# A three-layer kernel on one core: when weights are decoded, how the last part of `wo` is multiplied, and where weight parts are kept

## The chip, the cores and the metric

The kernel runs on one core of a Trainium2 chip. The metric is the device time of one execution in microseconds. Five engines of the core matter here: TensorE (PE) multiplies, VectorE (DVE), ScalarE (ACT) and GpSimd (POOL) work on tiles elementwise, and SyncE (SP) starts the transfers. Each engine takes its instructions strictly in the order in which they were written, and waits on semaphores for the others.

## The reference

Three steps follow each other, for 2 batches of 448 tokens:

```
scores = q @ k.T / 8, causal mask, softmax, @ v          # 12 heads of 64, per batch
x  = attn / sqrt(mean(attn^2) + 1e-6) * rms_g            # 896 x 768
x  = (silu(x @ w_gate) * (x @ w_val)) @ w_out            # 768 -> 1536 -> 768
y  = relu(x @ w_in)^2 @ w_out2                           # 768 -> 2048 -> 768
```

The weights come as 64-bit floats and the result is a 32-bit float.

## The kernel before, in words

**Numbers.** A weight tile (128 x 768 of 64-bit words, tile `raw`) is decoded on the core: ACT makes the exponent part (L639) and the lowest bits (L644), DVE puts the number together (L649). Then each 32-bit weight and each activation is split in two parts for PE: the high part is a rounded copy (L267 on ACT, L265 on POOL) and the low part is the rest (a subtraction: L676 for weights, on DVE or POOL; L559 for activations). A split weight of three 128 x 128 blocks lives in one of the buffers `ring`, a split activation in a `part`. One product of blocks is three matmuls (high x high, high x low, low x high), so a product of three blocks is 9 matmuls of 128 x 448 (L691).

**Products.** Each layer's matrix products work on pairs of output columns and both batches. `halves` does a pair with seven block products in place of eight (Strassen-Winograd): 7 x 9 = 63 matmuls, with sums of weight quarters (`minus`, L703, tiles `st`) and sums of activation quarters (`differences`, L723) in front, and additions behind. `whole` does a pair of output columns in the plain way: 2 columns x 2 batches x 2 x 9 = 72 matmuls. `wg` and `wv` (gate and value, ten `halves` after two plain columns), `wo` in two halves of its depth, then `w2i` (eight `halves`) and `w2o` follow.

**Attention.** Twelve pairs of heads run first. Per pair PE makes scores (L359, L363, L372, L375) in two PSUM tiles `s`, DVE takes maxima (L405, L403), ACT exponentials (L430), DVE reciprocals (L445, L446), POOL multiplies the rows (L456), PE transposes (L472), ACT or DVE copies the transposed rows out of PSUM (`pt<-t`, L308), and PE multiplies by the values (L505, L510). The squares of the result are summed (L535, L540) for the norm, whose column sums are PE's L573 and whose row broadcast is L592. The first four weight tiles of `wg` and `wv` are decoded while the attention runs, into the tiles `wt`. Their matmuls for batch 0 (L895) use the PSUM tiles of the scores.

**Order.** All work is given to a planner (class `Order`) as steps with a due time, the engines that may do it and how long each takes. The planner goes through time in its own model: it takes the step that can begin first, and of those within SLACK of it the one that is due first. A step with a choice goes to the engine on which begin + duration + COST is least; DVE pays PORT in place of its COST where the step is marked `port` (both operands in SBUF, which DVE and POOL are not planned to do together) and is not yet close to due (EASY, EARLY). SOON is how much earlier than a product's due time the step that clears its bank is due. What the planner leaves is a fixed order on each engine; on the chip only semaphores decide when an instruction runs.

Of the kernel before, what the change touches and what calls it, by code (L numbers as in the profile page):

```python
# [8 lines left out]
F32 = mybir.dt.float32  # L9
F32R = mybir.dt.float32r  # L10
BF16 = mybir.dt.bfloat16
U32 = mybir.dt.uint32
# [5 lines left out]
B, H, S, D = 2, 12, 448, 64  # L18
DM, DF1, DF2 = 768, 1536, 2048
P = 128  # L20
CP = 64
NCH = S // CP
NCC = DM // P
NF1 = DF1 // P
NF2 = DF2 // P
NPAIR = H // 2
# [3 lines left out]
CN = 112  # L30
NE = 2
STRIDE = 5.5
SLACK = 0.1
SWITCH = 0.1
SOON = 12.0
COST = {"D": 0.4, "P": 0.4}
PORT = 1.0
EASY = 1015
EARLY = 8
LAT = {"S": 0.0}  # L40
NEXT = 0.05
SPARE = 0.15
# [144 lines left out]
def tile_attention_moe_moe2(ctx: ExitStack, tc: tile.TileContext, qk, v, wg, wv, wo, w2i, w2o, rms_g, out):  # L187
# [16 lines left out]
    pw = ctx.enter_context(tc.tile_pool(name="pw", bufs=1))  # L204
# [5 lines left out]

    shapes = dict(raw=([P, 6 * P, 2], U32), wt=([P, 6 * P], F32), st=([P, 3 * P], F32), ring=([P, 6 * P + 64], F32R),
                  snap=([P, S], F32), tt=([P, S], F32), uu=([P, S], F32), part=([P, 2, S], F32R), row=([P, S], F32),
                  s=([P, 1024], F32))
    order = Order(dict(qk=3, v=3, p1=2, p2=2, pt=2))
    add, chain, buf = order.add, order.chain, order.buf

    def have(pool, **n):
        for name, k in n.items():  # L220
            for _ in range(k):
                i = len(order.places.get(name, ()))

                def make(name=name, i=i):
                    t = pool.tile(shapes[name][0], shapes[name][1], tag=f"{name}{i}", name=name, bufs=1)
                    if name == "ring":

                        o = 63
                        t = t[:, o:o + 6 * P].rearrange("p (a k n) -> p a k n", a=2, k=3)
                    return t  # L230

                order.more(name, make)

    def banks(name, *which):
        for i in which:
# [2 lines left out]
    have(psum, s=2)  # L238
    banks("t", 0, 1, 2)
    banks("o", 3)  # L240
    have(pw, raw=2, wt=2, st=4, ring=8)
    have(pt_, snap=5, tt=2, uu=2, part=6, row=14)


# [35 lines left out]
    for i, fill in enumerate((1.0, -1.0e9 * float(D) ** 0.5)):  # L280
        for k in range(2):
            for sl in (slice(0, D), slice(D, P)):
                t = half[sl, 2 * i + k]
# [8 lines left out]
    for i in range(NV):  # L292
        t = atc.tile([P, 4, 2 * D], F32, name=f"vt{i}")
# [3 lines left out]
    for i in range(2):  # L297
        t = atc.tile([P, 2, 512], F32, name=f"p2t{i}")
# [251 lines left out]
    def parts(src, due, prev=(), bs=None):  # L550

        bf, t, new = src[0], src[1], [] if bs else [buf("part")]
        bs = bs or new[0]

        def high(e):
            rnd(E(e), bs.tile[:, 0], bf.tile)

        def low(e):
            E(e).tensor_sub(bs.tile[:, 1], bf.tile, bs.tile[:, 0].bitcast(F32))  # L559

        t = add(due, {"A": A_(S), "P": P_(S)}, high, [t], new=new, uses=[bf] if new else [bf, bs], prev=prev)
        return bs, add(due, {"P": P_(S, True), "D": D_(S)}, low, [t], uses=[bf, bs], port=True)
# [235 lines left out]
    hf = [[None] * NF1, [None] * NF1]  # L798
# [107 lines left out]
        have(p, part=18, row=18)  # L906

    add(0.0, {"X": 0.0}, rows_come, used)
    norm(0, (NPAIR + 3.5) * STRIDE, 8.0)
    norm(1, 0.0, 0.3)  # L910
    ws = []
    for k in range(2 * NE):
        due = 40 + 8.0 * k
        c, t = weights((wg, wv)[k % 2][k // 2], NCC, due, due, "wt")
        ws.append([form((c, o, t), 3, due) for o in (0, 3 * P)])
    whole_tiles(0, ws, 1000.0)
# [8 lines left out]
    due = 1020.0  # L925
# [36 lines left out]
    def halved(x, k0, prev=(), both=False):  # L962

        x = [y[k0:k0 + NCC] for y in x]
        f = dict(B11=[parts(x[0][j], due - 6 + j, prev) for j in range(3)],
                 B21=[parts(x[0][j + 3], due - 5 + j, prev) for j in range(3)])
        f.update(differences(x, due - 4, prev, both))
        f.update(B22=[parts(x[1][j + 3], due + j + 6, prev) for j in range(3)])
        return f

    def highs(f):
        return [x[1] for y in (f.values() if isinstance(f, dict) else f) for x in y]
# [22 lines left out]
    def seven(src, k0, f, sums, due, last=False, n=NCC // 2):  # L995


        for a in range(n):
            c = (a, a + NCC // 2)
            own = [[sums[j][c[i]] for i in range(2)] for j in range(B)]  # L1000

            def done(i, j, bank, snap, after, due, keep, c=c, own=own):
                t = kept(own, i, j, bank, snap, after, due, c[i] if last else None)
                sums[j][c[i]] = own[j][i]
                return t

            halves(src[c[0]][:, k0:k0 + NCC], src[c[1]][:, k0:k0 + NCC], f, due, done,
                   sums=own if own[0][0] else None, end=last and a == NCC // 2 - 1)
            due += 12.8
        return due  # L1010

    def whole(src, k0, n, x, sums, due, a0=0):

        for a in range(a0, NCC):
            c = a // 2 + a % 2 * NCC // 2
            layer(src[c], x, k0, [n], due, lambda b, bank, t, due, c=c: kept(sums, c, b, bank, None, [t], due))
            due += 1.22 * n * 2
        return due
# [2 lines left out]
    g = halved(hf, 0, highs(f))  # L1021
    due = seven(wo, 0, g, yf, due)
    hx = halved(hf, NCC, highs(g))
    due = seven(wo, NCC, hx, yf, due, n=NCC // 2 - 1)
    hy = [[parts(hf[1][NCC + i], due - 5 + i, highs(hx)) for i in range(3)]]
    due = whole(wo, NCC, NCC, [hx["B11"] + hx["B21"], hy[0] + hx["B22"]], yf, due, NCC - 2)
    f = halved(yf, 0, highs(hy))
    h2 = [[None] * NF2, [None] * NF2]

    def squared(b, ft, bank, snap, after, due, keep=False):  # L1030
# [77 lines left out]
```

## Time and profile before

| what | value |
|---|---|
| runs before | 555.04, 553.03, 550.48 us; median 553.03 |
| profiled execution | 552.47 us, span 550.7 us, so 1.8 us lie around the span |
| mean granted clock of PE | 0.996 |
| busy in the span | PE 540.6, PE weight load 477.3, DVE 420.2, ACT 411.0, POOL 301.8 us |
| matmuls of L691 | 2115, 429.4 us busy |
| bytes | 65.06 MB by DMA, mean 118 GB/s |

A matmul's end in the trace is modelled, so PE's busy share hides short waits: what counts is when matmuls start. A row of the timeline merges instructions of one kind that follow each other without a wait, with the start of the first and their count; the time from one row's start to the next row's start is what they took in all.

### The profile page before, as it was taken

Reading aid. Unit: us, or ns where it says so; the run is one execution under the profiler, and the core shown is the slowest. Engines: PE = TensorE matmul, PEld = TensorE weight load, DVE = VectorE, ACT = ScalarE, POOL = GpSimd, SP = SyncE. Lnnn points to the kernel's source line nnn. Section 1 sums busy time; section 2 is a strip of 40 time slices with the busy share of each in tenths; the row PEclk is TensorE's granted clock in tenths of the full one; section 3 lists DMA queues with packets and bytes.
Section 4 is the critical chain, followed back from the end, with each engine's and each line's share of the span. In section 5 each row is a group of like instructions: output and inputs, shape, how many; then the busy total and the mean of one; then the engine's idle time right before and its main releaser. Section 6 shows DMA issues by size and latency. Waiting matters only on the chain.

```text
span 550.7 us, 8919 instructions
## 1 busy us (share of the span) xinstructions
PE 540.6 (98%) x3067; PEld 477.3 (87%) x3067; DVE 420.2 (76%) x781; ACT 411.0 (75%) x879; POOL 301.8 (55%) x338
## 2 busy tenths in 40 slices
PE   8999999999999999999999999999999999999997
PEld 5776666798899999999999989899899999999996
DVE  3667867699999897889867877996777544778883
ACT  3889989656867766679888776888887998659610
POOL 3555555325232372248999789231113897899810
PEclk9999989999999999999999999999999999999999
DMA  7246514023144333333544153243332343333422
GB/s 184 86 140 191 166 55 132 0 78 130 57 147 165 116 115 115 114 116 114 170 140 149 58 174 115 62 156 128 114 117 77 114 154 114 115 115 116 148 85 83
DMA packets 19501, 65.06 MB, mean 118 GB/s; under 512 B 2048, under 2 KB 8960, under 8 KB 19456
## 3 DMA queue, kind: packets, MB, share of 16 engines
q1 hardware_dynamic: 19376, 64.27, 35.8%
q8 instruction: 24, 0.39, 0.3%
q10 hardware_dynamic: 80, 0.23, 0.1%
q14 instruction: 21, 0.17, 0.1%
HBM read 61.74 MB, written 2.75 MB: 117 GB/s over the span
## 4 chain that ended last, share of the span: by engine, by line
PE 74%; DVE 13%; ACT 6%; DMA 3%; issue 2%; POOL 1%; POOLq 0%; DVEq 0%; ACTq 0%
PE m L691 61%; DVE part L559 3%; PE t L472 3%; PE o L510 3%; PE s L359 3%; DVE ring L676 2%; DMA raw<-in_w2i 2%; PE s L372 2%; DVE row L723 1%; PE s L895 1%; ACT ring L267 1%; ACT p2t L430 1%; DVE s L649 1%; POOL p L456 1%; ACT s L639 1%
## 5 line engine op out<-in xcount | busy, mean ns | idle before, releaser
L691 PE MATMUL m<-part,ring 128*128 128x448 f32 x2115 | 429.4, 365 | 1.4 <-ACT ring L267 0.6
L691 PEld LDWEIGHTS m<-part,ring 128*128 128x128 f32 x2115 | 396.9, 188 | 33.8 <-ACT ring L267 1.2
L559 POOL TENSOR_TENSOR part<-row,part 128x448 fp32r<-128x448 f32 x103 | 121.5, 1204 | 50.6 <-ACT part L267 47.3
L676 DVE TENSOR_TENSOR ring<-s,ring 128x384 fp32r<-128x384 f32 (+1 forms) x156 | 82.3, 541 | 39.1 <-ACT ring L267 38.3
L267 ACT CAST ring<-s 128x384 fp32r<-128x384 f32 (+1 forms) x156 | 71.5, 471 | 23.8 <-PE m L691 14.8
L267 ACT CAST part<-row 128x448 fp32r<-128x448 f32 x131 | 69.1, 571 | 6.8 <-DVE row L611 2.6
L723 POOL TENSOR_TENSOR row<-row 128x448 f32<-128x448 f32 x57 | 66.3, 1179 | 12.3 <-DVE row L835 11.4
L644 ACT ACTIVATE raw<-raw 128x768 uint32<-128x768 uint8 (+1 forms) x70 | 62.5, 895 | 13.9 <-DMA raw<-in_w2o 4.5
L265 POOL TENSOR_SCALAR ring<-st 128x384 fp32r<-128x384 f32 x14 | 7.4, 527 | 100.9 <-PE m L691 48.6
L639 ACT ACTIVATE s<-raw 128x768 f32<-128x768 f32 (+1 forms) x64 | 54.0, 853 | 7.9 <-DVE ring L676 6.4
L649 DVE SCALAR_TENSOR_TENSOR s<-s,raw 128x768 uint32<-128x768 uint32 (+1 forms) x64 | 48.8, 762 | 10.9 <-ACT s L639 5.9
L676 POOL TENSOR_TENSOR ring<-st,ring 128x384 fp32r<-128x384 f32 x45 | 45.9, 1038 | 5.0 <-ACT ring L267 3.7
L456 POOL TENSOR_SCALAR p<-p,r 128x128 f32<-128x128 f32 (+1 forms) x48 | 24.0, 517 | 27.0 <-DVE r L446 25.1
L267 ACT CAST ring<-st 128x384 fp32r<-128x384 f32 x44 | 21.5, 515 | 23.0 <-DVE st L703 22.4
L405 DVE TENSOR_REDUCE mx<-s 128x2 f32<-128x256 f32 (+2 forms) x36 | 24.1, 688 | 17.9 <-PE s L375 11.2
L703 DVE TENSOR_TENSOR s<-s,st 128x384 f32<-128x384 f32 x56 | 31.6, 564 | 1.6
L456 POOL TENSOR_SCALAR p2t<-p2t,r 128x256 f32<-128x256 f32 (+1 forms) x36 | 23.1, 658 | 17.3 <-DVE r L446 7.3
L703 DVE TENSOR_TENSOR st<-st,s 128x384 f32<-128x384 f32 x56 | 30.5, 545 | 0.2
L359 PE MATMUL s<-qk 64*128 64x128 f32 (+2 forms) x144 | 26.4, 448 | 1.6 <-ACT p2t L430 1.1
L981 DVE TENSOR_TENSOR row<-m,row 128x448 f32<-128x448 f32 x36 | 22.3, 618 | 6.7 <-PE m L691 6.4
L308 ACT COPY snap<-m 128x448 f32<-128x448 f32 x43 | 22.8, 530 | 5.2 <-PE m L691 5.0
L559 DVE TENSOR_TENSOR part<-row,part 128x448 fp32r<-128x448 f32 x37 | 25.3, 708 | 0.9 <-ACT part L267 0.8
(101 smaller groups left out, 564.4 us busy)
## 6 DMA issues: line engine op xcount, KB each, us to landing
raw<-in_w2i SPq DMA_DIRECT2D x16, 768.0 KB, 4.2
raw<-in_wg SPq DMA_DIRECT2D x12, 768.0 KB, 4.5
raw<-in_wv SPq DMA_DIRECT2D x12, 768.0 KB, 4.3
raw<-in_wo SPq DMA_DIRECT2D x12, 768.0 KB, 4.3
raw<-in_w2o SPq DMA_DIRECT2D x12, 768.0 KB, 4.5
qk<-in_qk SPq DMA_DIRECT2D x11, 448.0 KB, 4.0
raw<-in_w2o SPq DMA_DIRECT2D x6, 512.0 KB, 3.7
out_t<-row SPq DMA_DIRECT2D x12, 224.0 KB, 1.9
```

Of the source, the lines that this page charges most:

```text
L267: eng.copy(o, i)
L359: nc.tensor.matmul(s[:, h, o:o + n], z["qk"][BOTH[h], 0, qs], z["qk"][BOTH[h], 1, :n], start=True, stop=False)
L405: nc.vector.tensor_reduce(z["mx"][:, k:k + 2], src, AX, ALU.max)
L456: E(e).tensor_scalar(t, t, z["r"][:, k:k + 1], 1.0, ALU.mult, ALU.mult)
L559: E(e).tensor_sub(bs.tile[:, 1], bf.tile, bs.tile[:, 0].bitcast(F32))
L639: nc.scalar.activation(bt.tile[:, :n * P], br.tile[:, :n * P, 1].bitcast(F32), AF.Prelu, scale=2.0 ** -112, alpha=2.0 ** 32)
L644: nc.scalar.activation(br.tile[:, :n * P, 0], b, AF.Copy, scale=1.0 / 32, bias=-31.0 / 64)
L649: nc.vector.scalar_tensor_tensor(dst.tile.bitcast(U32) if dst else u, u, 3, br.tile[:, a:b, 0], ALU.logical_shift_left, ALU.bitwise_or)
L676: E(e).tensor_sub(br.tile[:, 1, :n], num(), br.tile[:, 0, :n].bitcast(F32))
L691: nc.tensor.matmul(bank.tile[:, :S], bw.tile[:, a, i], x[:, c], start=first and i == 0 and k == 0, stop=last and i == n - 1 and k == 2, sk ...
L703: (E(e).tensor_add if plus else E(e).tensor_sub)(bs.tile[:, o:o + 3 * P], x, y)
L723: E(e).tensor_sub(bs.tile, a[0].tile, b[0].tile)
```

## The change

It has four parts. The planner's numbers are others (eight of them, and some due times). The four early weight tiles are due at 26, 41, 56 and 71 of the planner's time in place of 40, 48, 56 and 64, and the norm of batch 0 is due at 55 in place of 52.25. The last two columns of `wo`'s second half, before a `whole` of 72 matmuls, become a third `halves` of 63. There are nine buffers `ring` in place of eight, cut from one tile `rings`, and three tiles `st` in place of four.

```diff
-SLACK = 0.1
+SLACK = 0.15
...
-COST = {"D": 0.4, "P": 0.4}
-PORT = 1.0
+COST = {"D": 0.3, "P": 0.4}
+PORT = 1.1
...
-    have(pw, raw=2, wt=2, st=4, ring=8)
+    have(pw, raw=2, wt=2, st=3)
+
+    NR = 9
+    rings = pw.tile([P, NR * 6 * P + 64], F32R, name="rings")
+    for i in range(NR):
+        order.more("ring", lambda i=i: rings[:, 63 + i * 6 * P:63 + (i + 1) * 6 * P].rearrange("p (a k n) -> p a k n", a=2, k=3))
...
-    norm(0, (NPAIR + 3.5) * STRIDE, 8.0)
+    norm(0, (NPAIR + 4) * STRIDE, 7)
...
-        due = 40 + 8.0 * k
+        due = 26 + 15 * k
...
-    due = seven(wo, NCC, hx, yf, due, n=NCC // 2 - 1)
-    hy = [[parts(hf[1][NCC + i], due - 5 + i, highs(hx)) for i in range(3)]]
-    due = whole(wo, NCC, NCC, [hx["B11"] + hx["B21"], hy[0] + hx["B22"]], yf, due, NCC - 2)
-    f = halved(yf, 0, highs(hy))
+    due = seven(wo, NCC, hx, yf, due)
+    f = halved(yf, 0, highs(hx))
```

The lines of the kernel move up by three to five with it (L676 becomes L673, L308 becomes L305). Counted over the whole program PE has 9 instructions fewer, ACT 37 fewer, POOL 36 fewer and DVE 68 more; the transfers are the same 121. The moves between engines that make up these counts are: low parts of weights in `st` on POOL 45 before and 11 now, on DVE 13 and 49; copies `pt<-t` on ACT 41 and 20, on DVE 7 and 28; the last `relu` and square of `w2i`'s tiles on ACT (two instructions each) 23 and 10, on DVE (one) 9 and 22.

The first place is DVE in the middle of the attention, from a copy of a pair's result to the reciprocals of the next but one. Before:

```order
L308 COPY row<-o 128x448
L405 TENSOR_REDUCE mx<-s 128x2
L445 TENSOR_SCALAR r<-su 128x4
L446 RECIPROCAL r<-r 128x4
L403 TENSOR_REDUCE mx<-s 128x1
L308 COPY pt<-t 128x2x2x128
L405 TENSOR_REDUCE mx<-s 128x2
L540 TENSOR_TENSOR snap<-snap,tt 128x448
L405 TENSOR_REDUCE mx<-s 128x2
L445 TENSOR_SCALAR r<-su 128x3
L446 RECIPROCAL r<-r 128x3
```

And now:

```order
L305 COPY row<-o 128x448
L402 TENSOR_REDUCE mx<-s 128x2
L442 TENSOR_SCALAR r<-su 128x4
L443 RECIPROCAL r<-r 128x4
L400 TENSOR_REDUCE mx<-s 128x1
L305 COPY pt<-t 128x2x2x128
L305 COPY pt<-t 128x2x4x64
L402 TENSOR_REDUCE mx<-s 128x2
L537 TENSOR_TENSOR snap<-snap,tt 128x448
L402 TENSOR_REDUCE mx<-s 128x2
L442 TENSOR_SCALAR r<-su 128x3
L443 RECIPROCAL r<-r 128x3
```

DVE has taken a second copy `pt<-t` between the maxima, which ACT did before.

The second place is POOL in the stage of `wg` and `wv`, up to the nine differences for `wo`. Before:

```order
L265 TENSOR_SCALAR ring<-st 128x384
L676 TENSOR_TENSOR ring<-st,ring 128x384
L723 TENSOR_TENSOR row<-row 128x448 x2
L265 TENSOR_SCALAR ring<-st 128x384
L676 TENSOR_TENSOR ring<-st,ring 128x384
L265 TENSOR_SCALAR ring<-st 128x384
L676 TENSOR_TENSOR ring<-st,ring 128x384 x2
L265 TENSOR_SCALAR ring<-st 128x384
L676 TENSOR_TENSOR ring<-st,ring 128x384 x2
L723 TENSOR_TENSOR row<-row 128x448 x9
```

And now:

```order
L720 TENSOR_TENSOR row<-row 128x448
L556 TENSOR_TENSOR part<-row,part 128x448 x3
L720 TENSOR_TENSOR row<-row 128x448 x2
L262 TENSOR_SCALAR rings<-st 128x384 x2
L720 TENSOR_TENSOR row<-row 128x448 x9
L262 TENSOR_SCALAR rings<-st 128x384
L673 TENSOR_TENSOR rings<-st,rings 128x384
```

The subtractions for the low parts in `st` have left POOL here; they stand on DVE.

The third place is PE at the column sums of batch 0's norm. Before, they stand between the scores of the tenth pair:

```order
L363 MATMUL s<-both 128x64
L573 MATMUL o<-ones,snap 112x1 x4
L359 MATMUL s<-qk 128x256 x2
```

```order
L472 MATMUL t<-ident,p_968 128x128 x8
L505 MATMUL o<-pt,vt_119 64x128 x2
```

And now, one pair earlier, in front of a transpose:

```order
L360 MATMUL s<-both 128x64
L570 MATMUL o<-ones,snap 112x1 x4
L469 MATMUL t<-ident,p_864 128x128 x8
L502 MATMUL o<-pt,vt_118 64x128 x2
L507 MATMUL o<-pt,vt_118 64x320 x4
L507 MATMUL o<-pt,vt_118 64x192 x2
L507 MATMUL o<-pt,vt_118 64x64 x2
L356 MATMUL s<-qk 128x256 x2
```

The sums moved from behind the eighth pair's transposes to behind the seventh's, and no scores follow them directly.

## Rows read from the trace of the kernel before

**Rows 1.** The page's first part: busy us (share of the span) and instructions by engine.

```profile
PE 540.6 (98%) x3067; PEld 477.3 (87%) x3067; DVE 420.2 (76%) x781; ACT 411.0 (75%) x879; POOL 301.8 (55%) x338
```

**Rows 2.** Busy time by stretch: length, then busy us (instructions) by engine, granted clock, DMA.

```profile
core 0: us, PE busy (x) PEld busy (x) DVE busy (x) ACT busy (x) POOL busy (x), PEclk, DMA share, GB/s
20.00:38.00 18.00, 18.00 (x185) 13.15 (x180) 10.61 (x26) 15.27 (x54) 9.13 (x18) 1.00 0.29 88
38.00:64.00 26.00, 25.10 (x248) 17.30 (x248) 19.96 (x43) 24.34 (x76) 14.45 (x27) 1.00 0.60 192
...
112.00:160.00 48.00, 47.52 (x236) 43.77 (x235) 47.83 (x87) 34.45 (x66) 18.84 (x16) 1.00 0.28 97
160.00:260.00 100.00, 100.00 (x499) 93.35 (x498) 87.47 (x157) 71.88 (x132) 41.43 (x42) 1.00 0.39 127
...
386.00:494.00 108.00, 107.81 (x523) 98.58 (x522) 68.58 (x126) 86.56 (x166) 69.81 (x66) 1.00 0.35 117
```

**Rows 3.** PE's timeline in the stream: start, us, instruction xcount [idle before <-releaser].

```profile
116.48 18.56 PE L691 MATMUL m<-part,ring 128*128 128x448 f32 x92
135.28 12.61 PE L691 MATMUL m<-part,ring 128*128 128x448 f32 x61 [0.24 <-DVE ring L676]
148.12 169.84 PE L691 MATMUL m<-part,ring 128*128 128x448 f32 x846 [0.23 <-ACT ring L267]
318.37 67.65 PE L691 MATMUL m<-part,ring 128*128 128x448 f32 x333 [0.41 <-ACT ring L267]
386.21 161.05 PE L691 MATMUL m<-part,ring 128*128 128x448 f32 x783 [0.19 <-ACT snap L308]
```

**Rows 4.** Busy time and counts of L691's matmuls alone, in two stretches of the stream.

```profile
268.00:308.00 40.00, 40.00 (x201) 37.56 (x200) 1.00 0.37 120
...
400.00:440.00 40.00, 40.00 (x195) 36.59 (x194) 1.00 0.32 106
```

**Rows 5.** PE's timeline at the value products of pairs two to six.

```profile
26.68 0.44 PE L505 MATMUL o<-pt,vt 128*64 128x128 f32 x4
...
33.58 0.44 PE L505 MATMUL o<-pt,vt 128*64 128x128 f32 x4
...
48.22 0.44 PE L505 MATMUL o<-pt,vt 128*64 128x128 f32 x4
...
54.39 1.22 PE L472 MATMUL t<-ident,p 128*128 128x128 f32 x8 [0.23 <-POOL p L456]
55.54 0.44 PE L505 MATMUL o<-pt,vt 128*64 128x128 f32 x4
```

**Rows 6.** PE's timeline from 71 us, behind the sums of batch 0's norm.

```profile
71.00 0.70 PE L359 MATMUL s<-qk 64*128 64x256 f32 x4 [1.10 <-ACT p2t L430]
...
71.71 1.89 PE L472 MATMUL t<-ident,p 128*128 128x128 f32 x8
73.53 0.69 PE L505 MATMUL o<-pt,vt 128*64 128x128 f32 x4
...
76.25 0.97 PE L372 MATMUL s<-qk 64*64 64x224 f32 x8
```

**Rows 7.** PE alone by stretches of 2 us: busy us (instructions), granted clock, DMA.

```profile
72.00:74.00 2.00, 2.00 (x12) 0.50 0.00 2
74.00:76.00 2.00, 2.00 (x16) 0.68 0.00 0
```

**Rows 8.** Groups by shape: busy us, mean ns of one | idle us before, by releaser.

```profile
L676 DVE TENSOR_TENSOR ring<-s,ring 128x384 fp32r<-128x384 f32 x150 | 80.9, 551 | 38.4 <-ACT ring L267 37.6
L676 DVE TENSOR_TENSOR ring<-st,ring 128x384 fp32r<-128x384 f32 x13 | 8.1, 650 | 0.0
L308 DVE COPY pt<-t 128x512 f32<-128x512 f32 x7 | 4.8, 680 | 1.1 <-PE t L472 1.1
L1044 DVE SCALAR_TENSOR_TENSOR row<-row 128x448 f32<-128x448 f32 x9 | 5.6, 619 | 0.2
...
L676 POOL TENSOR_TENSOR ring<-st,ring 128x384 fp32r<-128x384 f32 x45 | 45.9, 1038 | 5.0 <-ACT ring L267 3.7 <-PE m L691 0.2
```

More of the change, by code (lines that the diff above doesn't have):

```diff
@@ L32 @@
 STRIDE = 5.5
-SLACK = 0.1
+SLACK = 0.15
 SWITCH = 0.1
-SOON = 12.0
-COST = {"D": 0.4, "P": 0.4}
-PORT = 1.0
-EASY = 1015
-EARLY = 8
+SOON = 14.0
+COST = {"D": 0.3, "P": 0.4}
+PORT = 1.1
+EASY = 1020
+EARLY = 5
 LAT = {"S": 0.0}
@@ L209, in tile_attention_moe_moe2 @@
     atc = att.enter_context(tc.tile_pool(name="atc", bufs=1))
-    shapes = dict(raw=([P, 6 * P, 2], U32), wt=([P, 6 * P], F32), st=([P, 3 * P], F32), ring=([P, 6 * P + 64], F32R),
+    shapes = dict(raw=([P, 6 * P, 2], U32), wt=([P, 6 * P], F32), st=([P, 3 * P], F32),
                   snap=([P, S], F32), tt=([P, S], F32), uu=([P, S], F32), part=([P, 2, S], F32R), row=([P, S], F32),
@@ L222, in have @@
                 i = len(order.places.get(name, ()))
[L224 to L232, printed above, removed]
+                order.more(name, lambda name=name, i=i: pool.tile(shapes[name][0], shapes[name][1], tag=f"{name}{i}",
+                                                                   name=name, bufs=1))
     def banks(name, *which):
```

## The prediction, made before the changed kernel was run

> **What bounds the kernel now.** I read the page's first part, then the busy time by stretch, then PE's own timeline.
>
> The first part shows PE at 98% of the span, and no other engine over 76% [rows 1]. A matmul's end is modelled, so the 98% alone proves little. The timeline counts starts. From 116.48 us to the end PE runs one stream of 2115 matmuls, which waits only four times [rows 3]. Its longest part, 846 matmuls from 148.12 to 318.37 us, takes 201.2 ns for each. Nothing but fewer or denser matmuls shortens that. The last part is less dense without any wait: 783 matmuls in 161 us, 205.6 ns each, 3.4 us more than at 201.2. Inside it the same instruction of the same shape starts 195 times in 40 us, where an earlier stretch has 201, both at a granted clock of 1.00 [rows 4]. So PE has two cadences. The slower one began after the wait at 386.21 us, and no instruction of the program is special to it.
>
> The attention, up to about 105 us, has another limit. From one pair's value product to the next PE takes 33.58 - 26.68 = 6.90 us early on, and 55.54 - 48.22 = 7.32 us later, where it waits for POOL's row factors [rows 5]. In that later stretch ACT is busy 24.34 of 26 us (94%), in the earlier one 15.27 of 18 (85%), while DVE has 77% and 59% [rows 2]. The decoding of early weights has come on top of ACT's exponentials, and POOL waits at the end of that chain. Behind the norm's sums PE waits another 1.10 us for ACT's exponentials to free a PSUM tile [rows 6], and then its clock falls: 0.50 of full speed, which is its lower level of 1.2 GHz, over 72 to 74 us, and 0.68 as a mean over the next two [rows 7].
>
> **The change, part by part.** The sum starts from the profiled execution, 552.47 us; the median of the three runs, 553.03, is 0.6 above it, and I add nothing for that.
>
> *Seven products for the last two columns of `wo`.* 63 matmuls in place of 72: 9 x 0.2012 = 1.8 us less on PE [rows 3], on the path since the stream is dense. What it costs is work elsewhere: three more weight parts, four more sums of weights, three more additions behind the products, and less slack before `w2i`. Before, four products of the next pairs (36 matmuls, 7.2 us) lie in PE's order between the last product of `wo` and the first that needs all of its columns; now three (5.4 us). Over that time DVE has about ten instructions of 0.55 to 0.62 us in its order (the shapes of [rows 8]), 6 us at the middle. This could cost PE up to 0.7 us or nothing; I take nothing, since POOL and ACT share the chain.
>
> *The attention.* Decoding goes from one weight in 8 of the planner's units to one in 15, and 21 copies `pt<-t` go from ACT to DVE. At 680 ns each [rows 8] that is 14.3 us more on DVE over twelve pairs, 1.2 us in each pair's 6.9. DVE's 59% without decoding becomes some 76% by the copies and ACT loses about as much, so neither is near the 94% at which the waits stood. I count as gone: four pairs that took 0.42 us too long, 1.7 us; the wait of 1.10 us; and the time at the lower clock, (1 - 0.50) x 2 + (1 - 0.68) x 2 = 1.6 us [rows 5 to 7]. Together 4.4. The other bound is a loss: the norm's sums need the sixth pair's squares, and stand less than a pair's period behind its value product now, before more than one and a half. If nothing is won and PE waits here as it did for the exponentials, it is +1.1. I take -4.4, because the stretch from 20 to 38 us shows this very loop without waits at ACT's 85%.
>
> *Low parts from POOL to DVE.* 36 subtractions move; at 551 ns alone they are 19.8 us of DVE, against 36 x 1.038 us of POOL given back [rows 8]. In the stage of `wg` and `wv`, 12 of them move (13 stand on POOL there before, 1 now): 6.6 us. DVE's load from 112 to 260 us goes from 47.83 + 87.47 = 135.3 to 141.9 of 148 us [rows 2]: 96%, which fits, narrowly. What a full DVE does to PE is seen from 116.48 to 148.12 us, where DVE is at 99.6%: 153 matmuls take 31.64 us, 0.9 more than at 201.2 ns [rows 3]. Spread over 148 us this would be 4.1, of which 0.9 is there already. I take +1.5, between 0 and 3.2. In `w2i`'s stage DVE has 68.58 of 108 us [rows 2]; the 13 squares (619 ns) and some ten low parts add 14 us and stay at 76%, so I cost them at nothing, with DVE's own idle time as the cover.
>
> Beside this: `st,ring` on DVE takes 650 ns as a mean where `s,ring`, whose first operand lies in PSUM, takes 551 [rows 8]. The Trainium skill (GPSIMD Engine Reference, section Specifications) says that GpSimd shares its SBUF interfaces with VectorE and contends with instructions that read two SBUF operands, which speaks against this move. By that rule each moved subtraction is priced at the 650, and DVE would get 3.6 us more in all.
>
> *Nine buffers in one tile, three `st`.* One more buffer lets the parts run 9 matmuls further ahead. In the built program each write to a buffer waits for the matmul that read that same slice last, so the common tile couples nothing. The waits it can spare are among the four of the stream, and the tile `st` that is missing can cost as much. I put it at 0.
>
> *The cadence.* Each wait seems to draw it anew, and of four waits one led to the slow one. In the likeliest case the stream runs at 201 throughout and 3.4 us go; but the runs before spread over 4.6 us, so a median probably holds some of it. I take half, -1.7, with 0 and -3.4 as its near bounds.
>
> The sum: 552.47 - 1.8 - 4.4 + 1.5 - 1.7 = 546.1. I predict **546 us**, 1.3% below the median.
>
> **Rivals.**
>
> *The waits move with the work (22%).* The copies and the early decoding put DVE's reciprocals later, and POOL waits for those instead of for ACT. For it: POOL's factors need DVE's result, and DVE is in order. Against: 76% is far from 94%. Then the attention gives nothing: 552.5 - 1.8 + 1.5 - 1.7 = 550.5.
>
> *DVE becomes the bound (13%), slower than before.* Place: 112 to 260 us. DVE is already at 99.6% for the first 48 us, and the change brings it more backlog out of the attention. If its 12.5 us of idle time in 160 to 260 are waits that it can't fill, then the 12 moved subtractions lie on the path, 6.6 us, and the attention's gain is only backlog passed on: 552.5 - 1.8 + 6.6 = 557.3. It decides from the point where DVE's load reaches what PE takes, 12.7 us for 63 matmuls. The Trainium skill (Perfetto Trace Analysis, section Identifying the Most-Contended Engine) takes busy time as a fair measure for VectorE but not for matmuls, where the weight loads count. By that rule DVE (47.83 of 48 us) and not PE (43.77) is the engine to relieve from 112 to 160 us, and this rival would be the forecast; the trace agrees for 48 us only, since in the next 100 it has 87.47 against 93.35.
>
> *The stream falls into the slow cadence early (6%).* With few waits left there is nothing to end it. 195 against 201 starts is 3.1%, over 2106 matmuls 13.1 us, of which 3.4 are there now: 546.1 + 1.7 + 9.7 = 557.5.
>
> *The tile does couple its buffers (2%).* Every decoding would wait for the latest product: far above 600 us. The program's waits speak against it.
>
> **How the numbers follow.** The forecast has 57%, with 542 (all of the cadence, no price on DVE) to 550 as its own range. A measurement here can tell about 1% from no change: 547.5 and 558.6 are the bounds. Faster: three quarters of the forecast and a little of the first rival, 44%. Slower: a third of the two rivals at 557, and the last, 10%. The rest, 46%, is within 1%. The range that leaves out 2 in 10 goes from 541.5, a little under the forecast's best case since two waits of PE in the attention weren't counted, to 557.
>
> **What would show it.** The changed profile should have 2106 matmuls of 128 x 448 in the stream; pairs 6.9 us apart through the whole attention, with the first matmul of the stream 4 us earlier; no stretch of clock below 1 after the start; DVE near 96% from there for 150 us and PE without long waits on DVE's low parts; and 201 starts in any 40 us of the stream. I am wrong if PE's waits in the attention carry DVE's name, if the stream shows many waits for `rings` released by DVE, or if it starts 195 times in 40 us for long.

## The result and the profile after

The changed kernel is slower: **555.04 us** median of 20 runs, against 548.82 us for 20 runs of the kernel before that were taken beside it. The ratio is 1.0088, 95% interval 1.0065 to 1.0111. I had forecast 546. The ratio leaves out four of the 20 runs: 752 and 1857 us (mean granted clock 0.655 and 1.000; why is not known), and 559 and 561 us, which are over 1.5% above the fastest. The profiled execution took 555.26 us, that of the kernel before 552.47, which turns out to be one of its slower ones.

The page's first part, beside [rows 1]: DVE has 37 us more, ACT 19 and POOL 39 us less, and PE 4 us less.

```profile
PE 536.6 (97%) x3058; PEld 473.6 (86%) x3058; DVE 457.3 (83%) x849; ACT 392.3 (71%) x842; POOL 263.2 (48%) x302
```

Busy time by stretch, with the columns of [rows 2]:

```profile
38.00:64.00 26.00, 25.00 (x248) 17.58 (x248) 21.40 (x48) 22.87 (x75) 13.93 (x28) 1.00 0.48 157
112.00:160.00 48.00, 45.56 (x226) 41.98 (x225) 47.48 (x85) 31.57 (x61) 15.36 (x13) 1.00 0.24 83
160.00:260.00 100.00, 100.00 (x501) 93.91 (x501) 93.80 (x172) 72.85 (x136) 32.15 (x32) 1.00 0.39 130
```

DVE is full to 160 us as before, and at 94% behind it, where it had 87%. PE does not suffer in that second stretch: 100.00 of 100 us. It does in the first (45.56 for 47.52), and beyond 260 us. PE's timeline of the stream, beside [rows 3]:

```profile
114.00 26.81 PE L688 MATMUL m<-part,rings 128*128 128x448 f32 x133
141.72 2.47 PE L688 MATMUL m<-part,rings 128*128 128x448 f32 x11 [0.90 <-DVE part L556]
145.72 122.68 PE L688 MATMUL m<-part,rings 128*128 128x448 f32 x612 [1.54 <-DVE row L807]
270.21 88.28 PE L688 MATMUL m<-part,rings 128*128 128x448 f32 x432 [1.81 <-ACT snap L305]
359.41 136.01 PE L688 MATMUL m<-part,rings 128*128 128x448 f32 x657 [0.92 <-DVE row L1029]
495.60 22.21 PE L688 MATMUL m<-part,rings 128*128 128x448 f32 x108 [0.18 <-DVE row L763]
```

The stream starts 2.5 us earlier and then has waits of 0.9 to 1.8 us, where the longest of before was 0.41. The one at 270.21 is followed by a fall of the clock to its lower level:

```profile
270.00:274.00 4.00, 3.79 (x11) 3.39 (x12) 3.57 (x7) 2.90 (x7) 0.00 (x0) 0.57 0.22 35
```

The account comes from the start times of the stream's matmuls. I count what the intervals from start to start have over 200 ns, as *cadence* where one is under 225 ns, and as *waits* above that (the clock's fall included). In the profiled execution after against the one before, in us: start of the stream -2.5; nine matmuls fewer -1.8; waits 10.1 in place of 3.9, +6.2; cadence 4.5 in place of 3.7, +0.8. The sum is +2.7, and the stream's last matmul starts at 549.56 in place of 546.89; the ratio says +4.8, since the profiled execution of before is one of its slower ones. So one term has eaten the rest: **the waits**, 3.0 us around 141, 3.7 at 268, 1.2 at 358 and 2.2 from 495 on.

Where the 3.7 us come from is read off three engines. DVE, then POOL, then ACT, each from its own timeline:

```profile
261.88 0.56 DVE L700 TENSOR_TENSOR s<-s,st 128x384 f32<-128x384 f32 x1
262.34 1.43 DVE L832 TENSOR_TENSOR row<-row,uu 128x448 f32<-128x448 f32 x1
263.69 2.95 DVE L673 TENSOR_TENSOR rings<-st,rings 128x384 fp32r<-128x384 f32 x2
266.56 0.55 DVE L700 TENSOR_TENSOR s<-s,st 128x384 f32<-128x384 f32 x1
267.03 0.54 DVE L673 TENSOR_TENSOR rings<-s,rings 128x384 fp32r<-128x384 f32 x1
```
```profile
256.11 8.69 POOL L556 TENSOR_TENSOR part<-row,part 128x448 fp32r<-128x448 f32 x7
265.03 1.20 POOL L556 TENSOR_TENSOR part<-row,part 128x448 fp32r<-128x448 f32 x1 [0.24 <-ACT part L264]
```
```profile
267.66 0.48 ACT L264 CAST rings<-s 128x384 fp32r<-128x384 f32 x1 [2.71 <-DVE rings L673]
268.04 0.91 ACT L641 ACTIVATE raw<-raw 128x768 uint32<-128x768 uint8 x1
268.85 0.85 ACT L636 ACTIVATE s<-raw 128x768 f32<-128x768 f32 x1
269.64 0.52 ACT L305 COPY snap<-m 128x448 f32<-128x448 f32 x1
```

DVE's subtractions with an operand in PSUM (`s,st` and `s,rings`) take 0.55 us while POOL works, as ever. Those whose two operands lie in SBUF take 1.43, 1.52 and 1.51 us. In the records the last two end at 265.21 and 266.64, and the POOL instructions running when they started end at 264.79 and 266.23: 0.42 us earlier both times. So they didn't run slowly, they *waited until POOL's instruction was over*. That holds for all 15 `st` subtractions of this trace that begin while POOL has an instruction running (each ends 0.42 to 0.44 us behind it), while the 65 `s,rings` that begin so have a median of 548 ns against 549 elsewhere. The wait shows as a longer instruction and not as idle time in front of it, so it is not one for a semaphore; the sentence ahead of the prediction that only semaphores decide when an instruction runs does not hold here. Late in turn are DVE, then ACT, whose cast waits 2.71 us, and then PE, which waits for ACT's copy of a bank.

### The profile page after: what moved, and what is told of

The parts are those of the page before. It is cut to its first block, busy times and chain, and to the rows that moved or that the text cites. A ratio compares the mean times of both kernels' runs of the same rounds, so it can differ in the third digit from the quotient of the medians.

```text
span 553.3 us, 8904 instructions
## 1 busy us (share of the span) xinstructions
PE 536.6 (97%) x3058; PEld 473.6 (86%) x3058; DVE 457.3 (83%) x849; ACT 392.3 (71%) x842; POOL 263.2 (48%) x302
## 4 chain that ended last, share of the span: by engine, by line
PE 73%; DVE 14%; ACT 5%; DMA 4%; issue 2%; POOL 2%; POOLq 0%; ACTq 0%; DVEq 0%
PE m L688 58%; DVE rings L673 3%; PE o L507 3%; PE t L469 3%; PE s L356 3%; PE s L892 2%; DMA raw<-in_w2o 2%; DVE part L556 2%; PE s L369 2%; ACT rings L264 2%; POOL p L453 1%; DVE row L720 1%; ACT part L264 1%; DVE mx L402 1%; DMA qk<-in_qk 1%
## 5 line engine op out<-in xcount | busy, mean ns | idle before, releaser
L688 PE MATMUL m<-part,rings 128*128 128x448 f32 x2106 | 429.7, 366 | 6.2 <-ACT snap L305 1.8
L688 PEld LDWEIGHTS m<-part,rings 128*128 128x128 f32 x2106 | 395.9, 188 | 39.9 <-ACT snap L305 2.2
L556 POOL TENSOR_TENSOR part<-row,part 128x448 fp32r<-128x448 f32 x100 | 117.3, 1198 | 50.9 <-ACT part L264 49.6
L673 DVE TENSOR_TENSOR rings<-s,rings 128x384 fp32r<-128x384 f32 (+1 forms) x157 | 82.2, 541 | 21.9 <-ACT rings L264 21.0
L264 ACT CAST rings<-s 128x384 fp32r<-128x384 f32 (+1 forms) x157 | 70.1, 477 | 16.4 <-DVE s L646 5.3
L720 POOL TENSOR_TENSOR row<-row 128x448 f32<-128x448 f32 x57 | 69.1, 1230 | 20.1 <-DVE row L832 18.6
L262 POOL TENSOR_SCALAR rings<-st 128x384 fp32r<-128x384 f32 x12 | 6.2, 516 | 113.4 <-DVE st L700 79.5
L264 ACT CAST rings<-st 128x384 fp32r<-128x384 f32 x48 | 23.1, 514 | 26.3 <-DVE st L700 19.9
L673 DVE TENSOR_TENSOR rings<-st,rings 128x384 fp32r<-128x384 f32 x49 | 32.0, 685 | 0.0
L305 ACT COPY snap<-m 128x448 f32<-128x448 f32 x46 | 24.6, 535 | 7.5 <-PE m L688 7.0
L556 DVE TENSOR_TENSOR part<-row,part 128x448 fp32r<-128x448 f32 x37 | 27.7, 764 | 0.7 <-ACT part L264 0.6
```

The lines of the kernel that those rows point to most:

```text
L264: eng.copy(o, i)
L673: E(e).tensor_sub(br.tile[:, 1, :n], num(), br.tile[:, 0, :n].bitcast(F32))
L688: nc.tensor.matmul(bank.tile[:, :S], bw.tile[:, a, i], x[:, c], start=first and i == 0 and k == 0, stop=last and i == n - 1 and k == 2, sk ...
L720: E(e).tensor_sub(bs.tile, a[0].tile, b[0].tile)
```

## The experiments

The theories, with the letters that the expectations use. A: the numbers' low parts of `st` on DVE make the loss; A1: each waits for POOL, and the chain above leads to PE; A2: DVE's load delays PE at 140 us. B: the missing `st` tile or the nine buffers. C: the cadence is drawn by each execution. L, W, N are told where they come. For every kernel I also counted, from 100 us on, DVE's `st` subtractions that began while POOL worked and took over 0.62 us, and the time they lost so ("`st` waits"), in the one execution that was profiled. Numbers alone, engine prices alone and the numbers in the attention only had four runs each, the others of the table ten or more.

| kernel | ratio to before, 95% | `st` low parts on DVE | `st` waits, us |
|---|---|---|---|
| before | 1 | 13 | 1.2 |
| changed | 1.0088 [1.0065, 1.0111] | 49 | 6.5 |
| numbers alone | 1.0109 [1.0050, 1.0169] | 53 | 11.3 |
| all but the numbers | 1.0000 [0.9972, 1.0028] | 11 | 0 |
| seven products alone | 1.0051 [1.0014, 1.0087] | 16 | 0.8 |
| nine buffers, three `st`, alone | 1.0057 [1.0025, 1.0089] | 11 | 0.5 |
| due times alone | 1.0014 [0.9985, 1.0042] | 12 | 1.8 |
| engine prices alone | 1.0176 [1.0118, 1.0234] | 51 | 13.8 |
| changed, numbers in the attention only | 1.0067 [1.0015, 1.0118] | 13 | 0 |
| changed, nine low parts on POOL | 1.0044 [1.0013, 1.0075] | 40 | 1.2 |

### Which part

*Numbers alone*: the kernel before with six constants changed. (These six are all that the change sets, not eight as said ahead of the prediction.)

```diff
-SLACK = 0.1  SOON = 12.0  COST D 0.4  PORT = 1.0  EASY = 1015  EARLY = 8
+SLACK = 0.15 SOON = 14.0  COST D 0.3  PORT = 1.1  EASY = 1020  EARLY = 5
```

> The kernel before with the planner's six numbers alone (SLACK 0.15, SOON 14, COST of DVE 0.3, PORT 1.1, EASY 1020, EARLY 5). They move 40 low parts and 20 copies to DVE by themselves. Theory A (the loss comes from DVE's load): 3 to 8 us slower than before, waits of the stream near 140 us and where POOL has its long run of activation parts, with DVE over 95% busy from 112 to 160 us. Theory B (the loss comes from the missing tile st and the nine buffers): within 2 us of before. Theory C (the loss is the stream's slow cadence and luck): within 2 us once 6.7 ns for each matmul of the slow stretch are taken off.

*All but the numbers*: the changed kernel with the six old constants (the same diff backwards).

> The changed kernel with the planner's six numbers of before; the due times of the early weights, seven products, nine buffers and three st stay. Low parts on POOL 49, on DVE 11. Theory A: 3 to 6 us faster than before (1.8 for the nine matmuls, 2 or more in the attention), stream without waits over 1 us. Theory B: as slow as the changed kernel, 4 to 6 us over before. Theory C: either, with the slow stretch in it as long as in the changed kernel.

The numbers alone are slower by 1.1%, as A expected. All the rest is worth nothing either way: B's 4 to 6 us over before are out, and A's 3 to 6 us of gain did not come either. PE's stream in the kernel without the numbers has no wait for 979 matmuls:

```profile
115.97 196.22 PE L696 MATMUL m<-part,rings 128*128 128x448 f32 x979
312.79 17.42 PE L696 MATMUL m<-part,rings 128*128 128x448 f32 x83 [0.59 <-DVE part L564]
```

*Seven products alone*, *nine buffers and three `st` alone*, *due times alone*:

```diff
-    due = seven(wo, NCC, hx, yf, due, n=NCC // 2 - 1)
+    due = seven(wo, NCC, hx, yf, due)
```

> The kernel before with seven products for the last two columns of wo alone. Theory A: 1 to 2 us faster (nine matmuls of 201 ns, 1.8 us), at most 0.7 us of it lost at the start of w2i. Theory B: the same. A rival for the wo part itself: the additions behind the last products come too late, PE waits over 1 us at the start of w2i, and nothing is left of the 1.8 us.

```diff
-    have(pw, raw=2, wt=2, st=4, ring=8)
+    have(pw, raw=2, wt=2, st=3)
+    NR = 9
```

> The kernel before with nine buffers in one tile and three tiles st alone. Theory A: within 2 us of before. Theory B: 3 to 6 us slower, with waits of the stream that carry the sums of weights or their parts. If the common tile changes the cadence of the matmuls, the slow stretch covers much more or much less than a quarter of the stream.

```diff
-            due = 40 + 8.0 * k
+            due = 26 + 15 * k
```

> The kernel before with the new due times of the decoding ahead and of the norm alone (no seven products, no ninth buffer, old numbers). The order has 12 low parts of st on DVE, as before, and 9 of the softmax's copies on DVE, as before. If the due times are what moves the attention: stream starts at 114 and the kernel is 1 to 2.5 us faster than before (ratio 0.996 to 0.998). If they move little without the new numbers: start at 116, as in the kernel with all but the numbers, ratio 0.998 to 1.002. If they are what makes the changed kernel slower: ratio 1.005 or more.

Each of the first two is about 0.5% slower by itself, against A's expectation (1 to 2 us faster, and within 2 us); the second alone lies in B's range. The third is no change, and the three together cost nothing. These parts don't add; each makes the planner write another order. In the profiled execution of seven products alone, the longest of its ten runs, PE waits 2.1 us at 338.5, where the stage of `w2i` begins (for an ACT cast, then for a DVE low part): the transition that I priced at nothing has a wait in that order. In the changed kernel it has none. Whether this wait makes the 0.5% is not shown. B falls as the cause of the 0.9%, since these parts are all there in the kernel of ratio 1.0000.

*Engine prices alone*: only COST, PORT, EASY and EARLY of the diff above.

> The kernel before with the prices of the engines alone (COST of DVE 0.3, PORT 1.1, EASY 1020, EARLY 5), SLACK and SOON as before. It moves 38 low parts to DVE but only one copy of the attention. Theory A (low parts on DVE make the loss): 3 to 6 us slower than before, as with all six numbers. Rival (SLACK and SOON, with the copies of the attention, make it): within 2 us of before.

The worst of all, 1.8% or 9.6 us where A expected 3 to 6, with the most `st` waits: 18 subtractions lose 13.8 us. Its `st` low parts take 822 ns as a mean, against 650 before [rows 8].

*The changed kernel, with the new numbers for the steps of the attention only*:

```diff
-        return COST.get(e, 0.0)
+        return (COST_A if t["due"] < 1000 else COST).get(e, 0.0)
```

> The changed kernel with the new planner numbers only for steps due in the attention, and those of before for everything after. Low parts on POOL 47, copies on DVE 28 as in the changed kernel. Theory A: the attention's gain of 2.5 us and the 1.8 us of the nine matmuls are kept and the waits of the stream are those of before, so 3 to 5 us faster than before. Rival (the gain of the attention is only backlog passed on to the stream's start): waits over 2 us near 140 us all the same, within 1 us of before.

No `st` waits, and yet 0.7% slower, where A expected 3 to 5 us faster: the new numbers in the attention cost something of their own. It is at the start of the stream: its 201st matmul ("matmul 201" below) starts at 158.57 us, and at 155.97 in the kernel with all but the numbers, which differs from this one by them alone. The rival's waits near 140 us came, 3.1 us in all.

### The wait for POOL

The next kernels keep the changed kernel's order of steps and issue named steps to another engine.

```diff
-            t["f"](e)
+            t["f"](OVER.get(t["i"], e))
```

*The two low parts at 263.69 to POOL.*

> The changed kernel with every instruction in the same order, except that two low parts of st are issued to POOL in place of DVE: the two that take 1.51 us each on DVE at 263.7 and 265.1 us while POOL works on activations. Theory A1 (DVE held by POOL at the SBUF port starts the chain that ends in PE's wait at 268 us): that wait, 3.7 us with the half clock behind it, shrinks below 1 us, and the median falls by 2 to 4 us. Rival: POOL, busy until 268.8 us, becomes late itself and PE waits as long there.

The wait at 268 is gone; in its place stand two of 0.4 and 0.9 us, at 277 and 281, and the profiled execution takes 551.8 us in place of 555.3. The ratio, 1.0047 [0.9983, 1.011], says little with three runs, but A1 holds at its place.

*23 low parts to POOL, all those on DVE up to 266 us.*

> The changed kernel with every instruction in the same order, except that the 23 low parts of st in the stage of wg, wv and the step to wo are issued to POOL in place of DVE. Theory A2 (DVE's load also makes the waits at 140 us, where DVE is busy 11.96 of 12 us): those two waits, 3.0 us together, shrink to 1 us or less as four of the 23 stand in front of them, 2.2 us of DVE; with A1 the median falls by 4 to 6 us, to about that of before. Rival: the waits stay, since the backlog comes out of the attention and its end.

The wait at 268 is gone, those at 133 and 142 stay at 3.7 us. So A2 falls: taking the low parts off DVE does not shorten the wait at 140. (DVE's other steps met POOL's longer work there: its waits for POOL from 104 to 160 us are 6.5 us in place of 4.4.) The ratio, 1.009 [1.002, 1.016], is no better.

*The changed kernel once more, nothing changed.*

> The changed kernel once more, nothing changed, for one look. If the cadence of the matmuls (200, 203 or 207 ns from start to start) is drawn by each execution: the same waits of PE as in the profiled execution of the changed kernel within 0.3 us each, but another number of slow starts than 655 of 2106, in other stretches, and a span that differs by the 5 to 7 ns of each. If the cadence belongs to the order: again some 655, from 360 to 495 us.

This execution took 560.5 us and shows the mechanism at its largest. DVE at 304.37, POOL, PE behind it, and PE's clock:

```profile
303.90 0.56 DVE L700 TENSOR_TENSOR s<-s,st 128x384 f32<-128x384 f32 x1
304.37 5.03 DVE L673 TENSOR_TENSOR rings<-st,rings 128x384 fp32r<-128x384 f32 x1
309.32 0.61 DVE L763 TENSOR_TENSOR row<-m,row 128x448 f32<-128x448 f32 x1
```
```profile
291.97 17.01 POOL L556 TENSOR_TENSOR part<-row,part 128x448 fp32r<-128x448 f32 x15
```
```profile
271.65 35.21 PE L688 MATMUL m<-part,rings 128*128 128x448 f32 x171 [1.38 <-ACT snap L305]
309.98 10.32 PE L688 MATMUL m<-part,rings 128*128 128x448 f32 x36 [3.13 <-DVE row L763]
```
```profile
310.00:314.00 4.00, 4.00 (x11) 3.57 (x12) 1.67 (x4) 1.82 (x3) 0.00 (x0) 0.50 0.00 0
```

One subtraction of 0.55 us takes **5.03 us**: POOL runs fifteen low parts without a gap, the subtraction starts during the eleventh, and DVE gets its turn only behind the last, 0.42 us after its end at 308.98. PE waits 3.1 us, then runs at the lower level of its clock, 6.2 us in all. In the profiled execution above the same places read:

```profile
303.97 0.78 DVE L673 TENSOR_TENSOR rings<-st,rings 128x384 fp32r<-128x384 f32 x1
```
```profile
291.66 17.82 POOL L556 TENSOR_TENSOR part<-row,part 128x448 fp32r<-128x448 f32 x15
```
```profile
304.28 1.50 POOL L556 TENSOR_TENSOR part<-row,part 128x448 fp32r<-128x448 f32 x1
```

There POOL's run was as long and ended no earlier, at 309.47. But DVE came in behind the one instruction that was running, which ended at 304.34, and POOL's next, the last row above, took 1.50 us in place of about 1.17. So the same program loses 0.2 us or 4.5 us of DVE at one instruction. The long wait is the exception. In the profiles of all 17 kernels and repeats 152 `st` subtractions on DVE begin during a POOL instruction, 89 of them with POOL's next instruction right behind it; 150 end 0.41 to 0.54 us behind the one that was running. The two others are this one and the one at 305.6 below. And the long wait seems to have no part in the 1.0088: the fall of the clock behind it brings the mean granted clock of these two executions to 0.994 and 0.990, while the runs from which the ratio comes have 0.996 to 1.000.

The expectation that the waits are the same within 0.3 us failed here, and at 268 too, where PE's wait was 1.6 us, without a fall of the clock.

*Nine low parts to POOL*, those that lost most: the pairs near 189, 263, 304, 492 and the one at 519.

> The changed kernel, same order, but nine low parts of st are issued to POOL: the pairs near 189, 263, 304 and 492 us and the one at 519, which took up to 5.0 us on DVE while POOL worked. Theory L: the waits of 3.7 us at 268 and, in the executions that have it, of 6.2 us at 306 go; ratio 1.000 to 1.004 instead of 1.0088. If the cause of the loss is elsewhere (fewer transfers ahead, attention, cadence): 1.007 to 1.011.

551.06 us, ratio **1.0044 [1.0013, 1.0075]** in place of 1.0088. Where the two subtractions stood DVE now goes on, and the 3.7 us at 268 are gone from PE:

```profile
263.38 0.56 DVE L703 TENSOR_TENSOR s<-s,st 128x384 f32<-128x384 f32 x1
265.01 0.56 DVE L676 TENSOR_TENSOR rings<-s,rings 128x384 fp32r<-128x384 f32 x1 [1.07 <-ACT rings L267]
```
```profile
146.23 135.69 PE L691 MATMUL m<-part,rings 128*128 128x448 f32 x675 [1.51 <-DVE row L810]
282.46 74.11 PE L691 MATMUL m<-part,rings 128*128 128x448 f32 x369 [0.54 <-ACT snap L308]
```

The fall of the clock seems gone from every run: all 12 have a mean granted clock of 0.999 or 1.000, where 10 of the changed kernel's 18 runs from 550 to 561 us have 0.996 or 0.997, like the profiled one with its fall at 270. So about half of the loss goes with these nine low parts, a little less than L expected (1.000 to 1.004). The intervals of the two ratios overlap, from 1.0065 to 1.0075, so the half is a middle value. The nine also take 5 us of work off DVE; that it is the wait and not the work rests on the place at 268, and on the next kernel.

*The engine prices alone, and the POOL partners of its 18 late subtractions to DVE*; then *the 18 subtractions to POOL instead*.

> The kernel with the engine prices alone (1.018 times the kernel before), same order of steps, but the 18 POOL steps during which a low part of st on DVE started late in its profile are issued to DVE. Theory L (a DVE subtraction of two SBUF tiles that starts while POOL works waits until POOL's instruction has ended, and these waits, 14 us of DVE in that kernel, are what the prices cost): DVE gets 18 instructions more (18 x 0.55 = 9.9 us) and loses most of 14 us of waits; the kernel gets faster, ratio 1.007 to 1.013, and low parts of st over 1.3 us go from 12 to 3 or fewer. Theory W (DVE has too many instructions, the length of a few does not matter): slower, ratio 1.025 or more. If neither matters: 1.0176 +- 0.004.

> The kernel with the engine prices alone, same order, but the 18 low parts of st that started late on DVE are issued to POOL (18 x 1.04 us there). Theories L and W both: faster, since DVE loses 14 us of waits and 10 us of work; ratio 1.000 to 1.008, unless the low part stands behind POOL's own run of instructions and comes later than from DVE: then 1.0176 or more, and PE's waits in the stream stay at 10 us.

The first gave 1.0140 [1.0089, 1.0192], where 18 more instructions on DVE (10 us) should have made it slower if their count mattered. `st` waits fell from 13.8 to 5.8 us only, and five subtractions over 1.3 us were left, where L expected at most three. W's 1.025 lies outside the interval, so W is out at this place. The interval takes in 1.0176, though, so L's gain is not shown here. The second gave 1.0073 [1.0039, 1.0106], 1.0% better than 1.0176, with 1.8 us of `st` waits left.

### The start of the stream

*Five POOL steps between 110 and 137 us to DVE.*

> The changed kernel with the same order of steps, but five steps of POOL between 110 and 137 us (three differences of rows and two low parts of parts) are issued to DVE. In the changed kernel five DVE subtractions that start while one of these five runs take 0.43 to 0.97 us longer than their like (4.2 us in all), and each ends 0.48 us after POOL's instruction has ended. Theory L (DVE bounds the stream's start, and part of its time there is waiting for POOL's instruction): DVE gets five instructions more (5 x 0.53 = 2.7 us) and loses 4.2 us of waits, so the stream's matmul 201 comes 1.5 us earlier, at 155.5 us, although DVE has more to do. Theory W (DVE bounds there by the number of its instructions, the waits for POOL don't matter): matmul 201 comes up to 2.7 us later, at 159.7. Theory N (PE or the transfers bound there): no change, 157.0 +- 0.4. The rest of the kernel as it was: span 552 (L), 556 (W), 553 (N), up to the cadence of the matmuls, which differs by several us from one execution to the next.

Measured: matmul 201 at 157.78, that is 42.70 us after the stream's start, against 43.03 in both executions of the changed kernel. Five more instructions on DVE and 2.6 us less of waiting (4.4 to 1.8) come to nothing on balance, as 5 x 0.53 - 2.6 = 0.05 says: neither L's 1.5 us nor W's 2.7. By this number alone N, no change, fits as well; the next run speaks against N. This execution had a subtraction of 4.9 us at 305.6, too; the ratio was 1.0058 [1.0010, 1.0105].

*Four DVE subtractions issued twice.*

```diff
             t["f"](e)
+            if t["i"] in (665, 668, 700, 702):
+                t["f"](e)
```

> The changed kernel, but four DVE subtractions between 124 and 136 us (two low parts of weights from SBUF, two from PSUM) are issued twice in a row with the same result, 4 x 0.53 = 2.1 us more for DVE ahead of the waits of PE at 141.7 and 145.7. If DVE bounds the start of the stream: its first matmul still at 114.0, matmul 201 at 159.1 instead of 157.0. If PE or the transfers bound there, or the two waits come of POOL or ACT: 157.0 to 157.4.

Matmul 201 came at 158.03, where 159.1 was expected; but the stream started at 113.25 in this execution, so it came 44.78 us after the start, 1.75 later than in the changed kernel, of the 2.1 us put in. So, in the one execution that there is, DVE sets the pace there, nearly one to one. The counts of the stream's matmuls started by 160 us, before, changed, and the changed kernel once more, one view each:

```profile
L691 PE MATMUL m<-part,ring x212: 360/362/472, 116.5 to 159.8; 128*128 128x448 f32 x106
```
```profile
L688 PE MATMUL m<-part,rings x215: 360/362/472, 114.0 to 159.8; 128*128 128x448 f32 x108
```
```profile
L688 PE MATMUL m<-part,rings x211: 361/362/477, 115.0 to 160.0; 128*128 128x448 f32 x106
```

A start that is 1.5 to 2.5 us earlier leaves +3 or -1 matmuls at 160 us. The attention's gain is handed back within 45 us. The kernel with all but the numbers, whose stream starts at 116.0, has 221 by then. Its matmul 201 comes 40.00 us after its start, that of the kernel with nine low parts on POOL 43.03 us: these 3.0 us are nearly all that the stream of the latter takes longer, 429.0 us from its first matmul to its last against 425.9.

## Why the prediction was wrong

**The step that failed is "Low parts from POOL to DVE".** It priced the move by DVE's load: +1.5 us between 112 and 260, and nothing in `w2i`'s stage, "with DVE's own idle time as the cover". The load was right (93.80 of 100 us for a forecast of about 94) and PE bore it without a wait from 160 to 260. What cost is a low part that waits for POOL in front of a matmul that needs it, at 268 above all (3.7 us, and 1.6 in another execution), which no idle time of DVE elsewhere covers. That place is in `wo`'s stage, for which the sum had no term of this move: behind 260 us it went on to `w2i`. It also put `w2i` at 386 to 494 us, while the sums of `w2i`'s tiles (L1034 before, L1029 now) run from 343 to 445. I had the sign of the wait in hand, 650 ns as a mean for `st,ring` against 551 [rows 8], and read it as a price of 0.1 us per instruction, 3.6 us in all. It was 13 instructions of which three had lost 1.2 us; in the changed kernel twelve lost 6.5, up to 1.0 each. A mean of 0.1 hid single waits for most of a POOL instruction, which a dense PE sees as a late operand. The Trainium skill (SBUF — State Buffer, sections Terms and Who interferes with whom) states the rule that I should have weighed: VectorE with two SBUF inputs and GpSimd reading SBUF lock each other out, for the full instruction of the one that came first. The trace agrees for one instruction (1.52 us, 0.42 behind POOL's end); the 5.03 us behind five of them in a row go beyond that sentence.

The measured 555.04 lies inside my range of 541.5 to 557, but that is the second rival's doing, not the sum's.

**The attention.** Forecast -4.4 at the stream's start, measured -2.5 and -1.5. Inside the loop the size held, in part by luck: from the first pair's value product to the twelfth's PE takes 79.0 us, before 83.3, but 2.4 us of these 4.3 came at the twelfth pair, where I had forecast nothing. And 0.6 us more are spent before the first of them (1.6 in the second execution), and 1.2 more between the last and the stream. The wait of 1.10 us at 71 and the fall of the clock at 72 to 76 are gone (all engines, with the columns of [rows 2]):

```profile
72.00:74.00 2.00, 2.00 (x27) 1.35 (x23) 0.69 (x2) 2.00 (x10) 1.49 (x3) 1.00 0.09 33
```

The pairs near 70 are 6.90 us apart. But POOL's waits remain at 39 and 47 us, among the 0.42 us each that I had counted as gone (PE's timeline, beside [rows 5]):

```profile
39.37 0.89 PE L469 MATMUL t<-ident,p 128*128 128x128 f32 x5 [0.23 <-POOL p L453]
...
46.70 1.22 PE L469 MATMUL t<-ident,p 128*128 128x128 f32 x8 [0.23 <-POOL p L453]
...
63.52 0.44 PE L502 MATMUL o<-pt,vt 128*64 128x128 f32 x4
...
70.42 0.44 PE L502 MATMUL o<-pt,vt 128*64 128x128 f32 x4
```

More to the point, whatever is won there is worth little, since DVE bounds the next 45 us. My second rival said so ("only backlog passed on") about the same stretch, and that half of it is what happened. Its other half, 6.6 us of moved subtractions on PE's path from 112 to 260 us, did not, so that its 557.3 is close to the measured time is in part luck.

**Seven products.** Right: 2106 matmuls, 1.8 us of work. In some orders the gain is lost elsewhere: seven products alone came out slower, at 1.0051.

**The cadence.** Forecast -1.7, measured +0.8, but it isn't the change's. It was between +0.1 and +8.5 us in the profiles of these experiments, +4.5 and +5.1 in two executions of one program, with the slow stretches in other places. C stands as a source of spread, not of the difference. So 195 starts in 40 us, which came from 400 to 440 us, was no sign of being wrong: the kernel before has it too [rows 4].

**The base.** I summed from 552.47 us, and the median of 20 runs is 548.82: 3.7 us of the miss were in the three runs that I started from. The steps alone said -6.4 us; the measured difference is +4.8 by the ratio.

What stays open: the other half of the 0.9%. The 3 us of waits around 141 remain in each variant of the changed kernel that keeps the new numbers in the attention, come with these (1.0067 with the other parts and the old numbers behind the attention), and are absent without them. That DVE has no time left there is shown, which of its work is the needless part is not. No version beat the kernel before; the best, all but the numbers, equals it.

## What to carry to other kernels

Before moving elementwise work from GpSimd to VectorE, look for VectorE instructions with both operands in SBUF that start while GpSimd runs, and price each by what is left of GpSimd's instruction, up to the whole of it (a run of five was met twice in 152), not by the mean. Then look at which matmul needs the result: at 268 us three such waits of 0.8 to 1.0 us became 3.7 us of TensorE, while the stretch from 160 to 260 us, with DVE 94% busy, cost TensorE nothing. Keep such a step on GpSimd's own queue, or choose an operand in PSUM. A gain ahead of a stage is worth only what the stage's own bound lets through, so read the busy share of the *next* 50 us before counting it.

## What the runs showed of the hardware

A VectorE subtraction of two SBUF tiles that starts during a GpSimd instruction ends 0.41 to 0.54 us behind that instruction, in 150 of 152 cases and also where GpSimd's next instruction is right behind (1.51 us at 265.13). In the two others it waited for five GpSimd instructions in a row, to the end of GpSimd's run (5.03 and 4.92 us in two executions; 0.78 for the same subtraction in a third, inside a run as long). What decides between these was not found. GpSimd waits as well: one of its low parts took 1557 ns in place of 1160 while VectorE's subtraction ended.

The same matmul at a granted clock of 1.00 starts every 200, 203 or 207 ns, for hundreds in a row, and differently in two executions of one program. From 208 to 248 us the changed kernel had, in its first and its second profiled execution, 200 and 202.5 ns as a mean:

```profile
L688 PE MATMUL m<-part,rings x201: 361/362/365, 207.8 to 247.8; 128*128 128x448 f32 x101
```
```profile
L688 PE MATMUL m<-part,rings x199: 361/365/445, 207.8 to 247.9; 128*128 128x448 f32 x199
```

In the second it changed behind one interval that was 0.08 us longer, at 218.8.
